# Where the third-block sums of the seventh up group stand in a Strassen-Winograd MLP: before or behind the second down unit's left sums

## Chip, core and metric

One core of one Trainium2 chip. The metric is device microseconds of one execution; the kernel before takes 881.0 us, the median of 3 runs (880.43 to 881.81). The engines are named as in the profile: PE (matrix products) with its weight loads PEld, DVE (elementwise), ACT (activations, copies, and a DMA queue of its own), POOL, and SP, which only issues DMAs.

## What is computed

Routing attention, then a squared-ReLU MLP on its output. In the reference, cut to what matters:

```
x = attn_out.transpose(0, 2, 1, 3).reshape(3072, 512)   # 4 batches of 768 tokens
h = x @ w_in                                            # 512 x 2048
r = np.maximum(h, 0.0)
g = r * r
return (g @ w_out).astype(np.float32)                   # 2048 x 512
```

The attention runs in about the first 320 us and the change does not touch it. Everything below is the MLP.

## The kernel before, in words

**Stages.** The MLP handles the 4 batches one after the other, as n = 0, 1, 2, 3. Each has an *up* part (x @ w_in, ReLU, square, giving the tile `g`) and a *down* part (g @ w_out). The loop that calls them is at L1409 ff.: n = 0 uses `first_up` and `first_down`; n = 1, 2, 3 use `up` (L890) and the class `Down` (L1122), whose `run` (L1255) writes the order of the work out by hand. No scheduler reorders it: every engine executes its own instructions in the order in which the program issues them, and so do the DMA queues of SP and ACT. An instruction that waits holds up all that is behind it on its engine.

**Fast products.** Both matrix products are done by a Winograd form of Strassen's scheme: seven products of half-size operands instead of eight, for which sums and differences of the operand blocks have to be made first. The sums of the left operand `g` are made by DVE. In `up`, the 16 row blocks of the hidden dimension are made in F2 = 8 groups (i = 0 to 7), each giving four blocks c11, c12, c21, c22 of `g`. The "seventh group" is i = F2 - 2 = 6, and the last is i = 7.

**Two kinds of sums of a finished group f.** A batch's 768 tokens are two halves of 3 blocks of 128.
- `first_level(g, f)` (L1088) makes the sums over the first two token blocks (columns `TWO`): a `plus` and two `sub` of 128x256. The down units of this batch use them.
- `third_sums(g, n, f)` (L1100) deals with the third token block (columns `THIRD`): a `plus` and three `sub` of 128x128 into a tile `third`, which a DMA then stores to `g_far[n]` in DRAM (L1109). For f < 7 it first calls `store_third` (L1095), which stores the third block's own parts of `g` by one or, for even n, two DMAs. The third blocks of two batches (0 with 1, 2 with 3) are multiplied together in the down part of the odd batch, which reads them back from `g_far` by `load_left` (L1147).

`up` calls these for each group a group or two after it is made. For the seventh group `first_level` runs in the last group, and its `third_sums` is the very last thing that `up` issues (L971-972); the closure that would store the `third` tile is put on a list. For the last group (f = 7) `first_level` is the first line of `Down.run`, and `third_sums` comes in the first unit.

**Units of the down part.** `Down.run` goes through 7 units (n = 2) or 14 (n = 1 and 3, the third blocks of two batches being units of their own, `of` = 1). A unit is one half-size product, itself done by seven quarter-size products (`times`, L1111), each of 4 matmuls into a slice of a PSUM bank. In the trace one such matmul shows as 2 records, so that a quarter product is a row of x8. In a unit u, in this order:
- six quarter products on PE; behind the first, an ACT copy (L1270), and for u = 0 the stores of L1272-1273 on ACT's queue
- on DVE: the first step of the combination of the unit before (none for u = 0); then `sub(x[0][1], x[0][1], s[:, 1])` (L1282), which overwrites a left block with a difference
- the seventh quarter product on PE (L1283), whose left operand is that difference
- `load_right` for the next unit (L1286; four DMAs on SP into the four slots of `home`, each of which waits until PE has read its slot)
- `parts` (L1293): DVE makes the left sums of unit u + 1: a `plus` and two `sub` of 128x512
- for u = 0: `third_sums` of the last group, the left loads, the store of `third`
- the second step of the combination of the unit before

`parts` of the first unit is called in `up` already (`behind_seven`, L945). So at the seam between up and down DVE has, in this order: the last adds and the square of group 7, `third_sums(6)`, `first_level(7)`, the difference of L1282, the left sums of the second unit, `third_sums(7)`.

Of the kernel before, what the change touches and what calls it, by code (L numbers as in the profile page):

```python
# [25 lines left out]
def kernel(  # L26
# [10 lines left out]
    nc = tc.nc  # L37
# [849 lines left out]
        plus(middle, c34, middle)  # L887
        yield

    def up(b, g, n, x, behind_seven, stores):  # L890
        flat = g.rearrange("p f h n -> p (f h n)")
        odd = n == B - 1
        w_next = w_sums(0, odd)
        lefts, rights, done = {}, {}, []
        for i in range(F2):
            w, w_next = w_next, w_sums(i + 1, odd) if i + 1 < F2 else None
            ((c11, c12), (c21, c22)), product = group(i, g, w, x)
            ends, late = i >= F2 - 2, i % 2

            def result(j):  # L900
                bank = bank_tile(TB)
                product(j, bank)
                return bank

            def add(j, *results):
                bank = result(j)
                for out, to in results:
                    plus(out, bank, to)

            def levels_1():  # L910
                if done:
                    first_level(g, done[0])

            def levels_2():
                if done:
                    third_sums(g, n, done.pop(0))()

            def two():
                add(2, (c11, c11))
                square(c11)  # L920
                if i < F2 - 1:
                    levels_2()

            if i < 2:
                nc.scalar.copy(out=c11, in_=result(1))
            elif not late:
                next(unit_1)
                if ends:
                    load_right(1)
            if not (late or ends):  # L930
                lefts[4] = second_lefts(4, i)
            add(6, (c12, c11))
            if i < F2 - 1:
                levels_1()
            if i == 1:
                rights[1] = second_rights(1, x[0][0][0])
            if not late or ends:
                two()
            if i == 0:
                rights[4] = second_rights(4, x[4])  # L940
            add(7, (c21, c12))
            if ends:
                levels_1()
            if i == F2 - 1:
                behind_seven()  # L945
            r = spare_tile.rearrange("p i n -> p (i n)")
            if late and not ends:
                unit_4 = second(lefts.pop(4), rights[4], r, 0, TB)
                next(unit_4)
            add(5, (c22, c21), (c12, c12))  # L950
            square(c22)
            if i == F2 - 2:
                levels_2()
            if ends:
                sub(c21, c21, result(4))
            elif late:
                next(unit_4)
                unit_1 = second(
                    second_lefts(1, i + 1), rights[1], flat, 2 * TB * (i + 1), 2 * TB
                )  # L960
                next(unit_1)
                both = g[:, F2 + i - 1 : F2 + i + 1, 0]
                sub(both, both, r.rearrange("p (i n) -> p i n", i=2))
                for k in range(2):
                    square(both[:, k])
                two()
            add(3, (c12, c12))
            if ends:
                square(c21)
            (square if i < F2 - 1 else square_by_dve)(c12)  # L970
            if i == F2 - 1:  # L971
                stores.append(third_sums(g, n, i - 1))
            done.extend([i] if ends else [i - 1, i] if late else [])
        xT.pop(b)

# [119 lines left out]
    def store_third(g, n, f, queue=nc.sync):  # L1095
        queue.dma_start(g_far[n][f, :, 1:3], g[:, F2 + f, :, THIRD])
        if n % 2 == 0:
            queue.dma_start(g_far[n][f, :, 0], g[:, f, 0, THIRD])

    def third_sums(g, n, f):  # L1100
        if f < F2 - 1:
            store_third(g, n, f)
        a = block_of(g, f, THIRD)
        third = outp.tile([P, DM], F32, name="third", tag="osb").rearrange("p (j n) -> p j n", j=4)
        plus(third[:, 0], a[1][0], a[1][1])
        sub(third[:, 1], third[:, 0], a[0][0])
        sub(third[:, 2], a[0][0], a[1][0])
        sub(third[:, 3], a[0][1], third[:, 1])
        return lambda queue=nc.sync: queue.dma_start(g_far[n][f, :, 3:7], third)  # L1109

    def times(bank, left, rhs):  # L1111
        for f in range(F4):
# [8 lines left out]

    class Down:  # L1122
        def __init__(self, b, g, n):
            self.up_stores = []
            self.b, self.g, self.n = b, g, n
            both = n % 2
            self.units = (
                [(0, 1), (0, 4), (1, 4), (1, 1)] if both else [(0, 1), (0, 4)]
            ) + [(of, j) for j in RIGHT_ORDER[2:] for of in range(1 + both)]
            a = blocks(g, TWO)  # L1130
            s1, s2 = (s_home(i) for i in range(2))
            self.lefts = {
                1: a[0][0], 2: a[0][1], 3: s1, 4: a[1][1], 5: s1, 6: s2, 7: a[1][0]
            }
            self.a, self.s1, self.s2 = a, s1, s2
            self.count = 0
            self.stores = []
# [117 lines left out]
        def run(self):  # L1255
            first_level(self.g, F2 - 1)
            waiting = None
            for u, (of, j) in enumerate(self.units):
                x, s = self.ahead
                y = quarters(right(j))  # L1260
                copied = spare_tile[:, 4 + u % 2]
                one, two = (
                    bank_tile(4 * P).rearrange("p (i n) -> p i n", i=4) for _ in range(2)
                )

                ends = self.n == B - 1 and u + 1 == len(self.units)
                five = bank_tile(P) if ends else two[:, 3]
                last = bank_tile(P) if ends else None
                times(one[:, 0], x[0][0], y[0][0])
                nc.scalar.copy(out=copied, in_=one[:, 0])  # L1270
                if u == 0:
                    store_third(self.g, self.n, F2 - 1, nc.scalar)  # L1272
                    self.up_stores.pop()(nc.scalar)
                self.store()
                times(two[:, 0], x[0][1], y[1][0])
                times(two[:, 1], s[:, 1], slot(1))
                times(two[:, 2], x[1][0], slot(2))
                times(five, s[:, 0], slot(0))
                times(one[:, 2], x[1][1], slot(3))
                if waiting:  # L1280
                    next(waiting)
                sub(x[0][1], x[0][1], s[:, 1])  # L1282
                times(last if ends else one[:, 1], x[0][1], y[1][1])  # L1283
                if u + 1 < len(self.units):
                    if (k := self.units[u + 1][1]) != j:
                        load_right(k)  # L1286
                    if of and j in LATER:
                        self.load_left(LATER[j])
                    if self.n % 2 and u == 2:
                        self.load_left(5)  # L1290
                    if self.units[u - 1] == (0, 5):
                        sub(self.s1, self.a[0][1], self.s2)
                    self.parts()  # L1293
                if u == 0:
                    store = third_sums(self.g, self.n, F2 - 1)
                    self.find_results()
                    if self.n % 2:
                        self.load_left(4)
                        self.load_left(1)
                    store()  # L1300
                if waiting:
                    next(waiting, None)
                waiting = self.combine(of, j, one, two, five, copied, last)
                to_end = len(self.units) - 1 - u
                for kk in LOADS[self.n % 2].get(u, ()):
                    load_x(self.n + 1, kk)
                if to_end == 2 - self.n % 2:
                    sum_x(self.n + 1, 1)
                elif to_end == 0:
                    sum_x(self.n + 1, 2)  # L1310
            if self.n == B - 1:
                self.store(nc.sync)
            list(waiting)
            sum_x(self.n + 1, 1)
            self.store()
# [79 lines left out]
    x_summed = {}  # L1395
# [8 lines left out]
    for n, b in enumerate(FEED):  # L1404
# [12 lines left out]
            )  # L1417
        else:
            stage = Down(b, g, n)
            up(b, g, n, x_summed.pop(n)[-1], stage.parts, stage.up_stores)  # L1420
            stage.run()
    manual.close()
    fast.close()
# [190 lines left out]
```

## Time and profile before

| what | us |
|---|---|
| median of 3 runs | 881.0 |
| the profiled execution | 880.63 |
| its span (first to last instruction) | 878.8 |
| outside its span | 1.83 |
| PE busy | 870.7 (99% of the span) |
| DVE busy | 755.9 (86%) |
| ACT busy | 385.9 (44%) |
| POOL busy | 182.4 (21%) |

Up and down of n = 1 meet at about 512 us, those of n = 2 at 670 us, and those of n = 3 at 784.5 us. The profile gives for each row the engine, the line of the kernel and the operation, out<-in by tile names, shape and count. A bracket such as [1.39 <-DVE g L551] says how long the engine had been idle and what released it. Rows of matmuls have modelled ends; the distance from one start to the next is the better measure of PE's pace. SPq and ACTq rows are DMA issues by those engines' queues. The granted clock of PE in the profiled execution is 0.999 of full speed.

### The profile page before, as it was taken

The page shows a single profiled execution, that of the slowest core. Times are in us where ns is not written, and L with a number is a line of the kernel's source. Part 1 is how long each engine was busy: PE and PEld are TensorE (multiplying, and loading weights), DVE is VectorE, ACT ScalarE, POOL GpSimd, SP SyncE. Part 2 cuts the span into 40 slices and gives each one's busy share as a digit, 9 for nine tenths or more (in the row PEclk, how much of TensorE's full clock was granted, in tenths as well). Part 3 has the DMA queues.
Part 4 walks back from the last instruction along what each step waited for, and adds up shares of the span by engine and source line. Part 5 has one row for each costly group of instructions (what it writes and reads, how often), then busy time and mean ns, then how long its engine had stood idle before and what let it go on. Part 6 is the DMA issues. An engine that isn't in the chain of part 4 may idle for free.

```text
span 878.8 us, 14998 instructions
## 1 busy us (share of the span) xinstructions
PE 870.7 (99%) x5487; PEld 597.9 (68%) x5487; DVE 755.9 (86%) x1359; ACT 385.9 (44%) x621; POOL 182.4 (21%) x240
## 2 busy tenths in 40 slices
PE   9999999999999999999999999999999999999997
PEld 5444444444444455568866689997767977769997
DVE  6799888888888999999859986797899898997786
ACT  5877667777765657750034420002543015440000
POOL 0000010000000236740055300005540064500000
PEclk9999999999999999999999999999999999999999
DMA  7777786866764235226701347681024730147563
GB/s 253 175 188 202 214 267 177 209 181 194 203 168 124 83 139 172 89 95 227 277 25 43 101 145 217 186 258 37 31 91 148 240 116 25 37 134 230 166 203 124
DMA packets 166402, 136.05 MB, mean 155 GB/s; under 512 B 58826, under 2 KB 140082, under 8 KB 166066
## 3 DMA queue, kind: packets, MB, share of 16 engines
q1 hardware_dynamic: 148546, 118.67, 45.7%
q10 hardware_dynamic: 17776, 16.36, 5.9%
q8 instruction: 45, 0.74, 0.3%
q14 instruction: 35, 0.29, 0.1%
HBM read 82.10 MB, written 41.89 MB: 141 GB/s over the span
## 4 chain that ended last, share of the span: by engine, by line
PE 98%; DVE 0%; DMA 0%; ACT 0%; issue 0%; DVEq 0%
PE bank L793 28%; PE bank L1113 25%; PE sc L441 14%; PE av_a L475 10%; PE bank L1005 6%; PE av_b L475 5%; PE sc L450 4%; PE bank L883 3%; PE sc L329 1%; PE more L883 1%; PE sc L494 1%; PE more L873 1%; DMA q_raw<-in_q_dram 0%; PE av_a L289 0%; ACT ex L457 0%; PE av_a L274 0%
## 5 line engine op out<-in xcount | busy, mean ns | idle before, releaser
L457 ACT ACTIVATE ex<-sc 128x1024 f32<-128x1024 f32 x144 | 144.4, 1026 | 37.5 <-PE sc L441 31.6
L441 PE MATMUL sc<-qkT 64*128 64x512 f32 (+1 forms) x768 | 150.5, 484 | 0.0
L990 DVE TENSOR_TENSOR g<-bank,g 128x384 f32<-128x384 f32 (+3 forms) x205 | 102.2, 515 | 21.1 <-PE bank L793 12.5
L769 ACT ACTIVATE g<-g 128x384 f32<-128x384 f32 x122 | 63.0, 516 | 96.5 <-DVE g L990 75.2
L441 PEld LDWEIGHTS sc<-qkT 64*128 64x128 f32 x768 | 65.6, 188 | 42.1 <-issue 30.2
L793 PE MATMUL bank<-xT,w_s 128*128 128x384 f32 x256 | 93.1, 486 | 0.0
L793 PE MATMUL bank<-x_t,w_s 128*128 128x384 f32 x256 | 93.0, 486 | 0.0
L1270 ACT COPY spare<-bank 128x128 f32<-128x128 f32 x35 | 9.3, 264 | 187.9 <-PE bank L1113 149.7
L475 PE MATMUL av_a<-ex,v_raw 128*64 128x512 f32 x384 | 85.9, 596 | 0.0
L460 DVE TENSOR_TENSOR total<-total,ex 128x1024 f32<-128x1024 f32 x64 | 78.7, 1229 | 6.5
L161 POOL TENSOR_TENSOR w_in<-w_in,w_raw 128x512 int32<-128x512 int32 x16 | 21.5, 1341 | 294.4 <-DVE w_in L153 294.4
L571 POOL TENSOR_TENSOR w_s<-w_in 128x256 f32<-128x256 f32 x32 | 26.3, 821 | 247.4 <-PE bank L1113 146.5
L1113 PE MATMUL bank<-home,l 128*128 128x128 f32 x560 | 74.0, 275 | 0.0
L793 PEld LDWEIGHTS bank<-xT,w_s 128*128 128x128 f32 x256 | 48.6, 190 | 34.3 <-issue 0.6
L1113 PEld LDWEIGHTS bank<-home,l 128*128 128x128 f32 x560 | 68.2, 192 | 0.0
L793 PEld LDWEIGHTS bank<-x_t,w_s 128*128 128x128 f32 x256 | 48.1, 190 | 29.1
L793 PE MATMUL bank<-xT,w_in 128*128 128x384 f32 x184 | 67.1, 487 | 0.0
L770 ACT ACTIVATE g<-g 128x384 f32<-128x384 f32 x122 | 63.8, 523 | 3.9
L475 PEld LDWEIGHTS av_a<-ex,v_raw 128*64 128x64 f32 x384 | 26.1, 137 | 51.0 <-issue 49.7
L450 PE MATMUL sc<-rows 64*128 64x512 bf16 (+1 forms) x360 | 58.8, 323 | 0.0
L793 PEld LDWEIGHTS bank<-xT,w_in 128*128 128x128 f32 x184 | 34.4, 190 | 21.7 <-DVE g L551 0.6
L1113 PE MATMUL bank<-home,g 128*128 128x128 f32 x352 | 46.5, 275 | 0.0
(221 smaller groups left out, 1560.6 us busy)
## 6 DMA issues: line engine op xcount, KB each, us to landing
home<-w_far SPq DMA_DIRECT2D x92, 256.0 KB
words<-flat SPq DMA_DIRECT2D x26, 384.0 KB
w_raw<-in_moe_w_in_dram SPq DMA_DIRECT2D x16, 512.0 KB
w_raw<-in_moe_w_out_dram SPq DMA_DIRECT2D x16, 512.0 KB
w_far<-home SPq DMA_DIRECT2D x28, 256.0 KB
g<-g_far SPq DMA_DIRECT2D x28, 256.0 KB
v_raw<-in_v_dram SPq DMA_DIRECT2D x16, 384.0 KB
rb<-far_r SPq DMA_DIRECT2D x30, 192.0 KB
```

What stands on the lines that cost most here:

```text
L441: nc.tensor.matmul(sc[i][:, e, cols], lhsT=qkT[pair][rows, NCH + c], rhs=qkT[pair][rows, n.start // P : n.stop // P], start=first, stop=no ...
L450: nc.tensor.matmul(sc[i][:, e, cols], lhsT=ohT[pair][rows, 1, c * P : (c + 1) * P], rhs=ohT[pair][rows, 0, columns(i)], start=first, stop= ...
L457: nc.scalar.activation(out=ex[i], in_=sc.pop(i), func=ACT.Exp, scale=SCALE)
L460: eng.tensor_tensor(out=out, in0=a, in1=b, op=ALU.add)
L475: nc.tensor.matmul(bank[D * e : D * (e + 1), 0 : n.stop - n.start], lhsT=raw_v[pair][:, e, c], rhs=ex[i][:, e, cols], start=c == 0, stop=c ...
L769: nc.scalar.activation(out=to, in_=to, func=ACT.Relu)
L770: nc.scalar.square(to, to)
L793: nc.tensor.matmul(bank, lhsT=operands[j][0][:, kk], rhs=operands[j][1][:, kk], start=(kk == 0), stop=(kk == H2 - 1),)
L883: nc.tensor.matmul(bank, lhsT=left, rhs=right, start=True, stop=True)
L990: nc.vector.tensor_tensor(out=out, in0=one, in1=two, op=ALU.add)
L1005: nc.tensor.matmul(bank, lhsT=left[j][:, f], rhs=right(j)[:, f], start=(f == 0), stop=(f == F2 - 1),)
L1113: nc.tensor.matmul(bank, lhsT=left[:, f], rhs=rhs[:, f], start=(f == 0), stop=(f == F4 - 1))
```

## The change

```diff
-    def up(b, g, n, x, behind_seven, stores):
+    def up(b, g, n, x, behind_seven):
 ...
             (square if i < F2 - 1 else square_by_dve)(c12)
-            if i == F2 - 1:
-                stores.append(third_sums(g, n, i - 1))
             done.extend([i] if ends else [i - 1, i] if late else [])
 ...
     def third_sums(g, n, f):
-        if f < F2 - 1:
+        if f < F2 - 2:
             store_third(g, n, f)
 ...
-        return lambda queue=nc.sync: queue.dma_start(g_far[n][f, :, 3:7], third)
+        return lambda: nc.sync.dma_start(g_far[n][f, :, 3:7], third)
 ...
                 if u == 0:
-                    store_third(self.g, self.n, F2 - 1, nc.scalar)
-                    self.up_stores.pop()(nc.scalar)
+                    for f in (F2 - 2, F2 - 1):
+                        store_third(self.g, self.n, f, nc.scalar)
 ...
                 if u == 0:
-                    store = third_sums(self.g, self.n, F2 - 1)
+                    stores = [third_sums(self.g, self.n, f) for f in (F2 - 2, F2 - 1)]
                     self.find_results()
                     if self.n % 2:
                         self.load_left(4)
                         self.load_left(1)
-                    store()
+                    for store in stores:
+                        store()
```

In each of n = 1, 2, 3:
- On DVE the four instructions of `third_sums(6)` leave their place behind the square of group 7 and stand behind the left sums of the second unit, right ahead of the four of `third_sums(7)`. Nothing else moves on DVE.
- On ACT's queue the store of the sums of group 6 (256 KB) is gone; the stores of the third block's own parts of group 6 (128 KB, for n = 2 also 64 KB) are new, ahead of those of group 7.
- On SP's queue those stores of group 6 are gone from the end of `up`, and the 256 KB store of its sums is new, just ahead of the store of group 7's sums; for n = 1 and 3 both stand behind the left loads of L1298-1299.

PE's and POOL's instructions and their order are the same as before. The work done is the same in number and kind; one list and one argument go away.

More of the change, by code (lines that the diff above doesn't have):

```diff
@@ L1123, in __init__ @@
         def __init__(self, b, g, n):
-            self.up_stores = []
             self.b, self.g, self.n = b, g, n
@@ L1419 @@
             stage = Down(b, g, n)
-            up(b, g, n, x_summed.pop(n)[-1], stage.parts, stage.up_stores)
+            up(b, g, n, x_summed.pop(n)[-1], stage.parts)
             stage.run()
```

## The prediction

> **What bounds the kernel now.** I read the page's busy times first, then who waited for whom, then the chain that ended last from 700 us on, then the timeline at the three seams between up and down.
>
> The busy table and PE's waits in the whole MLP:
>
> ```profile
> PE 870.7 (99%) x5487; PEld 597.9 (68%) x5487; DVE 755.9 (86%) x1359; ACT 385.9 (44%) x621; POOL 182.4 (21%) x240
> ```
> ```profile
> PE bank L1113 <- DVE g L551: 1.4, 1, 1.4
> ```
>
> PE is the bound. Only what closes a gap in PE's stream can shorten the run, and the waits show just one gap in the MLP: 1.4 us, for a DVE subtraction. The chain shows where it lies, at the seam of n = 3 (start, us, what):
>
> ```profile
> 784.52 2.69 PE bank L1113 x24
> ...
> 787.21 0.56 DVE g L990
> ...
> 787.80 0.56 DVE g L773
> 788.36 0.21 DVE third L990
> ...
> 788.59 0.69 DVE third L551 x3
> 789.28 0.35 DVE home L990
> ...
> 790.52 0.70 DVE g L551
> 791.22 0.04 issue
> 791.27 82.47 PE bank L1113 x736
> ```
>
> Between the square of group 7 (L773) and `first_level(7)` (the "home" step) lie the four instructions that the change takes out. Behind them comes the difference of L1282 (790.52), which PE's seventh quarter product needs. From 791.27 to the end the chain is PE alone.
>
> Now the same place in the timeline, n = 3 and then n = 1:
>
> ```profile
> 788.27 0.28 DVE L990 TENSOR_TENSOR third<-g 128x128 f32<-128x128 f32 x1
> ...
> 788.82 1.06 PE L1113 MATMUL bank<-home,g 128*128 128x128 f32 x8
> ...
> 789.20 0.42 DVE L990 TENSOR_TENSOR home<-g 128x256 f32<-128x256 f32 x1
> ...
> 791.27 1.16 PE L1113 MATMUL bank<-w_out,g 128*128 128x128 f32 x8 [1.39 <-DVE g L551]
> ```
> ```profile
> 515.67 1.06 PE L1113 MATMUL bank<-home,l 128*128 128x128 f32 x8
> ...
> 516.56 1.06 PE L1113 MATMUL bank<-home,g 128*128 128x128 f32 x8
> 516.67 0.69 DVE L551 TENSOR_TENSOR g<-g,l 128x512 f32<-128x512 f32 x1
> ...
> 517.46 1.12 PE L1113 MATMUL bank<-w_out,g 128*128 128x128 f32 x8
> ```
>
> Quarter products start 0.892 us apart (786.14, 787.03, 787.92, 788.82 in n = 3). The seventh of n = 3 should start at 789.71 and starts at 791.27, so PE really loses 1.56 us (the row's 1.39 counts from a modelled end). In n = 1 it starts on time, at 517.46, but its weight loads start 0.96 us behind the ones before instead of 0.89: the difference ends at 517.36, just about when PE wants it. The loss is 0.07 us. The rows of n = 2 (675.47 behind 674.58, loads at 675.42 behind 674.47) give the same 0.07. So all that waits for DVE at the three seams is 1.56 + 0.07 + 0.07 = 1.70 us.
>
> **The four DVE instructions leave their place.** In n = 3 they reach from 788.27 to 789.20, start to next start: 0.93 us. Not all of that comes back. The first of them starts at 788.27, while the square before it (787.80, 0.56 long) still runs until 788.36; it doesn't depend on it. `first_level(7)` reads the square's result, and where one DVE instruction needs the one before it, the rows show a start 0.03 to 0.04 us behind its end (789.20 + 0.42 = 789.62, next 789.66). So it will start at 788.40, not at 788.27. It also waits for ACT's square of c22, done at 787.49. The gain is 789.20 - 788.40 = 0.80 us, not 0.93. Here the Trainium skill speaks otherwise: "VectorE: DVE Perf Modes", section "The DRAIN you can't avoid", says that each DVE instruction waits until the pipe is empty anyway, and that a semaphore between them costs nothing extra. By that rule order would not matter and the whole 0.93 would return; by the row a dependent start costs 0.13 us more than an independent one. I take the row: 0.80.
>
> The difference then ends at 790.41 instead of 791.21, and PE's seventh product starts at 790.47. **n = 3 gains 0.80**, and 0.76 of the stall stays; the same instruction is still what PE waits for. **n = 1 and n = 2 gain their 0.07 each**, all they have. The sum is 0.80 + 0.07 + 0.07 = **0.94 us**.
>
> **Where they go.** Behind the left sums of the second unit, DVE now has eight instructions of third-block sums instead of four. Those left sums end 0.80 earlier, so the first group stands in the hole: it starts near 792.26 (793.06 less 0.80) and the second group near 793.19 instead of 793.06, 0.13 late. Behind it stand the first combination (794.23 before, after 0.16 idle) and the difference of unit 1 (795.36 to 796.05). PE wants that difference at 791.27 + 7 x 0.892 = 797.51 before, and at 796.71 after. It should be there by about 796.0, so 0.7 us are spare and the cost is nothing. Without that cover, a delay d of DVE costs d - 0.7. In n = 1 and n = 2 the spare time is larger by the stall that they don't have there. From unit 2 on DVE waits for PE again (2.18 us at 806.76), so lateness doesn't pile up.
>
> Can the eight be slow there? The trace has slow ones: the group of n = 3 at 769.34 has instructions of 0.82 us instead of 0.28, beside sums on POOL that take 1.29 instead of 0.73 at 767.17. The Trainium skill ("SBUF — State Buffer", section "SBUF: two separate sides") calls the port pair that VectorE and GpSimd share an exclusive lock, which the loser waits for. By that rule, with POOL busy, a group would cost up to 4 x 0.82 = 3.3 us in place of 0.93, and the change would lose 1.7 us. But POOL's busy time is 0.00 from 784 to 800 us, and its next stage's sums wait for PE in the down part (93.9 us in n = 1). I take 0.93.
>
> **The queues.** SP loses the stores of group 6's own parts (781.77 in n = 3) and gains one 256 KB store. For odd n it stands behind the left loads, an issue of 0.5 us at 795.6 with SP idle until 801.39: nothing. For n = 2 the two stores go out at about 677.9 and 678.4, and `load_right` behind them is held by PE until 679.29 anyway; 256 KB at the 317 GB/s seen there is 0.8 us more traffic, while slot 1 is wanted at 678.21 + 6.25 = 684.46 and three microseconds are there. ACT's queue loses the wait for `third` (issue at 789.32) and gets one or two stores of 0.4 to 0.5 us; its next copy is due at 793.36, so 3 us cover that. The second left load at 794.10 overwrites what group 6's store still reads, so that store, now issued at 788.5 instead of 781.77, must have landed. The profile has that load wait 1.2 us for such a store (from about 790.7, so landed by 791.9) and then 2.2 us for `third_sums(7)`. One store more ahead moves 791.9 to 792.4, and the sums still come last. Bounds: zero gain, since nothing waits for an earlier issue, and at most 0.5 us of lateness. I take zero.
>
> Against the profiled execution: 880.63 - 0.94 = 879.69. The median of the runs is 0.37 above that execution, so 881.0 - 0.94 = **880.1**.
>
> **Rivals.** *A, more is hidden in the stalls.* The other executions may have DVE later at the seams than the profiled one, since the slow groups beside POOL vary (two slow instructions in n = 1, three in n = 3). n = 1 and n = 2 sit exactly on the edge, so any lateness there returns in full up to 0.80: at most 3 x 0.80 = 2.4, or 878.6; the 0.37 of the median alone would make it 879.7. Against it: 1.43 us of lateness that the profile doesn't show would have to be there. *B, the gain is given back.* The margin of 0.7 at unit 1's difference is used up, if the eight instructions or the copy before the combination come later than worked out. Then PE loses at unit 1 what it won at unit 0, and 880.9 results (the 0.14 of n = 1 and n = 2 remains). The row of the combination, which waited for PE and not for DVE, speaks against it. *C, slower: the second left load of the odd stages lands late*, because it now waits for a store issued 7 us later on another queue. It is wanted at 799.40 - 0.80 = 798.60 in n = 3; before, traffic restarts at 795.2 and its 256 KB are over by about 796.4. It decides if the load comes more than 2.2 us later, and makes the kernel slower in all from about 3 us; at 3.5 us n = 3 loses 1.3, n = 1 (3.1 of margin) 0.4, less the 0.94: 881.8. Against it is the wait for `third_sums(7)`, which comes after that store by nearly 2 us. That the change does not do what it says can be left out: the order of the instructions on DVE shows exactly the move.
>
> **Chances.** The forecast 0.60, A 0.22, B 0.12, C 0.06. A measurement of this kernel tells about 0.2% (1.8 us) from no change; 0.94 is 0.11%. Over that bound on the fast side lies about two thirds of A and a little scatter: 0.18. On the slow side half of C and scatter: 0.05. Within: 0.77. The range takes in most of A and all of B, with the runs' own scatter of 0.7: 878.9 to 881.2.
>
> **What would show it.** Right: at the seam of n = 3 the "home" row follows the square directly, about 0.04 us behind its end; PE's wait for "DVE g L551" falls from 1.39 to about 0.6; loads in n = 1 and n = 2 start 0.89 apart; the eight "third" rows stand together at about 0.28 each; no new wait on PE in units 1 and 2. Wrong: "third" rows of 0.8, a PE wait at unit 1's seventh product (B), or PE waiting for a DMA at the start of unit 2 (C); or a wait at that seam that has not changed, because DVE came to it later from the up part.

## The result

| | us, median | runs | lowest and highest |
|---|---|---|---|
| before | 880.64 | 17 | 879.89 to 881.81 |
| changed | 879.16 | 17 | 878.18 to 879.86 |

The ratio is 0.9982, interval 0.9975 to 0.9988: 1.48 us faster, and from 1.1 to 2.2 by the interval. The forecast was 0.94 us, to 880.1 (counted from the 880.64 measured here, 879.7); the range held the time. The sum was too small, and the profile shows where. The profiled execution of the changed kernel took 878.45 us, its span 876.7.

The busy table and the list of what PE waited for (us in total, times, longest):

```profile
PE 869.9 (99%) x5487; PEld 597.4 (68%) x5487; DVE 754.3 (86%) x1359; ACT 385.8 (44%) x621; POOL 181.7 (21%) x240
```
```profile
PE sc L179 <- DVE zeros L176: 1.1, 1, 1.1
PE av_a L274 <- DMA q_raw<-in_q_dram: 0.3, 1, 0.3
```

PE's wait for DVE at the seam is not smaller, it is gone; the two waits left are at the very start of the kernel. The chain that ended last now runs from the third seam to the end without a break (784 records in one piece, 736 and 24 with DVE between them before):

```profile
768.32 15.48 PE bank L793 x48
783.80 87.56 PE bank L1111 x784
```

The seam itself in the timeline of the changed kernel, n = 3 and then n = 1. L1111 is L1113 of before, L988 is L990:

```profile
783.64 1.95 PE L1111 MATMUL bank<-w_out,g 128*128 128x128 f32 x16
...
785.48 0.56 DVE L773 SCALAR_TENSOR_TENSOR g<-g 128x384 f32<-128x384 f32 x1
...
786.14 0.42 DVE L988 TENSOR_TENSOR home<-g 128x256 f32<-128x256 f32 x1
...
787.47 0.69 DVE L551 TENSOR_TENSOR g<-g,l 128x512 f32<-128x512 f32 x1
...
788.10 1.06 PE L1111 MATMUL bank<-home,g 128*128 128x128 f32 x8
...
789.00 1.06 PE L1111 MATMUL bank<-w_out,g 128*128 128x128 f32 x8
```
```profile
515.96 1.06 PE L1111 MATMUL bank<-home,g 128*128 128x128 f32 x8
...
516.86 1.06 PE L1111 MATMUL bank<-w_out,g 128*128 128x128 f32 x8
```

`first_level(7)` follows the square, as it should. In n = 3 the square starts 1.84 us behind PE's first down product (785.48 against 783.64). Before, it was 3.45 us: the square at 787.80, and PE's row

```profile
784.35 1.95 PE L1113 MATMUL bank<-w_out,g 128*128 128x128 f32 x16
```

So DVE came to the seam 1.6 us earlier *before it reached a single instruction that the change moves*. The difference of L1282 ends at 788.16, 0.8 us ahead of its use at 789.00.

### The profile page after: what moved, and what is told of

Its sections match the earlier page's. It is cut to its first block, busy times and chain, and to the rows that moved or that the text cites. A ratio compares the mean times of both kernels' runs of the same rounds, so it can differ in the third digit from the quotient of the medians.

```text
span 876.7 us, 14996 instructions
## 1 busy us (share of the span) xinstructions
PE 869.9 (99%) x5487; PEld 597.4 (68%) x5487; DVE 754.3 (86%) x1359; ACT 385.8 (44%) x621; POOL 181.7 (21%) x240
## 4 chain that ended last, share of the span: by engine, by line
PE 99%; DMA 0%; ACT 0%; DVE 0%; issue 0%
PE bank L793 28%; PE bank L1111 25%; PE sc L441 14%; PE av_a L475 10%; PE bank L1003 6%; PE av_b L475 5%; PE sc L450 4%; PE bank L883 3%; PE sc L329 1%; PE more L883 1%; PE sc L494 1%; PE more L873 1%; DMA q_raw<-in_q_dram 0%; PE av_a L289 0%; ACT ex L457 0%; PE sc L274 0%
## 5 line engine op out<-in xcount | busy, mean ns | idle before, releaser
L988 DVE TENSOR_TENSOR g<-bank,g 128x384 f32<-128x384 f32 (+3 forms) x205 | 102.3, 515 | 21.1 <-PE bank L793 12.8
L1111 PE MATMUL bank<-home,l 128*128 128x128 f32 x560 | 74.0, 275 | 0.0
L1111 PEld LDWEIGHTS bank<-home,l 128*128 128x128 f32 x560 | 68.2, 192 | 0.0
L1111 PE MATMUL bank<-home,g 128*128 128x128 f32 x352 | 46.5, 275 | 0.0
```

Source lines behind the costliest of these rows:

```text
L988: nc.vector.tensor_tensor(out=out, in0=one, in1=two, op=ALU.add)
L1111: nc.tensor.matmul(bank, lhsT=left[:, f], rhs=rhs[:, f], start=(f == 0), stop=(f == F4 - 1))
```

## Where DVE lost 1.6 us before, and why it no longer does

Followed back through the up part of n = 3, the traces first part in its group 3. Before, DVE stands idle for 0.46 us between two adds; with only the stores moved (`stores_only`, below) it is idle there for 0.10. The kernel before, then that one, whose second add is shown once more alone:

```profile
744.32 0.54 DVE L990 TENSOR_TENSOR g<-bank,g 128x384 f32<-128x384 f32 x1
745.32 1.02 DVE L990 TENSOR_TENSOR g<-bank,g 128x384 f32<-128x384 f32 x2 [0.46 <-PE bank L883]
```
```profile
744.31 1.67 DVE L990 TENSOR_TENSOR g<-bank,g 128x384 f32<-128x384 f32 x3
...
744.96 0.56 DVE L990 TENSOR_TENSOR g<-bank,g 128x384 f32<-128x384 f32 x1
```

From one add to the next it is 1.00 us before and 0.65 in stores_only, so DVE is 0.35 us late from there on. The bracket names PE, but PE's rows of the two kernels lie within 0.02 us of each other here, and in stores_only the same add starts 0.35 us sooner: PE is not what it waited for.

The 0.35 us grow in the next third-block sums. In the kernel before POOL starts first, in the changed kernel DVE does:

```profile
749.72 0.73 POOL L571 TENSOR_TENSOR w_s<-w_in 128x256 f32<-128x256 f32 x1 [1.73 <-PE bank L793]
...
749.89 0.70 DVE L990 TENSOR_TENSOR third<-g 128x128 f32<-128x128 f32 x1
...
750.63 0.78 DVE L551 TENSOR_TENSOR third<-third,g 128x128 f32<-128x128 f32 x1
```
```profile
748.82 0.28 DVE L988 TENSOR_TENSOR third<-g 128x128 f32<-128x128 f32 x1
749.00 0.73 POOL L571 TENSOR_TENSOR w_s<-w_in 128x256 f32<-128x256 f32 x1 [1.74 <-PE bank L793]
...
749.13 0.75 DVE L551 TENSOR_TENSOR third<-third,g 128x128 f32<-128x128 f32 x1
...
749.81 0.28 DVE L551 TENSOR_TENSOR third<-g 128x128 f32<-128x128 f32 x1
```

On time, DVE gets every second sum through between POOL's: 2 of 4 take 0.28 us. Late by 0.35, it meets POOL's sums in all four, and they take 0.70 to 0.82. Counted in the timeline, the up part of n = 3 has 8 sums of 0.6 us or more before (four in group 3, one in group 4, three in group 5) and 4 after (two each in groups 3 and 5). Row against row, DVE's delay against stores_only grows from 0.37 to 1.35 us in the sums of group 3 and to 1.89 with the one slow sum of group 4. It falls to 1.27 where stores_only is slowed in its turn, is back at 1.89 after group 5, and 1.61 at the seam. That is what turns 0.35 us into 1.6 us.

## The experiments

The table comes from each kernel's profile: slow sums (0.6 us or more) in the up part of n = 3, and the stall of PE at the third seam, which is the start of the seventh product less where four more steps of 0.892 put it. The ratio is to runs of the kernel before on the same chip. Slow sums and stalls are read from one profile of each kernel.

| kernel | us | ratio, interval | slow sums, n = 3 | third stall |
|---|---|---|---|---|
| before_again | 880.75 | 1.0001 (0.9993 to 1.0009) | 8 | 1.57 |
| sums_only | 879.22 | 0.9988 (0.9978 to 0.9998) | 4 | 0.00 |
| stores_only | 879.13 | 0.9982 (0.9976 to 0.9988) | 4 | 0.00 |
| double_seam | 883.55 | 1.0033 (1.0020 to 1.0046) | 4 | 0.89 |
| nudge_third | 879.56 | 0.9985 (0.9978 to 0.9992) | 4 | 0.00 |
| nudge_first | 879.60 | 0.9988 (0.9981 to 0.9994) | 4 | 0.01 |
| late_sums_first | 880.66 | 1.0000 (0.9992 to 1.0009) | 4 | 1.51 |
| late_sums_moved | 879.84 | 0.9991 (0.9983 to 1.0000) | 4 | 0.77 |
| pause_sums_first | 881.03 | 1.0002 (0.9994 to 1.0010) | 8 | 1.56 |
| pause_sums_moved | 880.09 | 0.9995 (0.9986 to 1.0004) | 8 | 0.84 |
| nudge_changed | 879.46 | 0.9984 (0.9977 to 0.9991) | 4 | 0.00 |
| after_again | 879.21 | 0.9981 (0.9974 to 0.9987) | 4 | 0.00 |

**Theories.** D: DVE's work at the seam delays PE one to one wherever DVE is late. Q: the gain comes from the queues. L: the third stall is an unlucky timing of DVE in the up part, which the change happens to break. A: a pause of half a microsecond is enough to start it.

**before_again**: no edit.

> The kernel before, unchanged, profiled once more. Theory D (DVE is late at the seam, and the stall comes back one to one where PE waits): the time is that of before, ratio 1.000 within 0.001, and the third seam again shows a stall of about 1.56 us. Theory L (the extra half microsecond of the gain, and the size of the third stall, is luck of how DVE meets POOL in the up part, different in every execution): the same time, but the third stall differs from 1.56 us by half a microsecond or more, together with the number of third-block sums of 0.7 us and more in the up part of n = 3 (7 or 8 in the first profile).

The pause is there again (745.43, 0.46 us), so are the 8 slow sums, and the stall is 1.57. So, as far as two profiles can tell, the lateness isn't drawn anew in each execution, as L had it: it belongs to this kernel.

**sums_only** and **stores_only** split the change.

```diff
 sums_only, against the changed kernel
+            if i == F2 - 1:
+                store_third(g, n, i - 1)
 ...
-                    for f in (F2 - 2, F2 - 1):
-                        store_third(self.g, self.n, f, nc.scalar)
+                    store_third(self.g, self.n, F2 - 1, nc.scalar)
```

> Only the four DVE instructions of group 6 move behind the second unit's left sums, and the store of their result with them; the stores of the third block's own parts of group 6 stay at the end of up on SP. Theory D: all of the gain, ratio 0.998 to 0.9985, no PE wait at the seams of n = 1 and n = 2. Theory Q (the gain comes from the queues: SP is free earlier, ACT waits for nothing): little or none of it, ratio 0.9995 to 1.000.

```diff
 stores_only, against before
-        if f < F2 - 1:
+        if f < F2 - 2:
 ...
-                    store_third(self.g, self.n, F2 - 1, nc.scalar)
-                    self.up_stores.pop()(nc.scalar)
+                    for f in (F2 - 2, F2 - 1):
+                        store_third(self.g, self.n, f, nc.scalar)
 ...
+                    self.up_stores.pop()()
                     store()
```

> Only the stores move, as in the change (group 6's own parts to ACT's queue, the store of the sums to SP behind the left loads); the four DVE instructions stay behind the square of group 7. Theory D: no gain, ratio 0.9995 to 1.0005, the third stall as in before. Theory Q: the gain of the change, ratio 0.998 to 0.9985.

*Each half gives about the whole gain.* D alone is wrong about stores_only, and Q alone about sums_only, whose third stall is gone too. By the medians the halves give 1.6 and 1.7 us, where both together give 1.5. (By its ratio sums_only gives 1.1 us, 0.2 to 1.9 by the interval; its time alone does not refute Q.) So the halves have something in common. What they share is in the table: 4 slow sums, no pause, no third stall. (They also share one edit, the store of group 6's sums on SP's queue; it is not the cause, since nudge_third below loses the stall without it and pause_sums_first has the stall with it.) In stores_only the four instructions still stand ahead of `first_level(7)`, and PE does not mind, because DVE is 1.6 us earlier. The difference between the halves is small: the down part of n = 1 is one piece of 87.54 us in sums_only and 87.61 in stores_only, that of n = 2 43.77 and 43.83. So the moved instructions are worth 0.07 and 0.06 us where DVE is on time, as forecast.

**double_seam**: the four instructions of group 6 made twice at their old place.

```diff
+        for _ in range(2 if f == F2 - 2 else 1):
             plus(third[:, 0], a[1][0], a[1][1])
 ...
```

> The kernel before with the four DVE instructions of group 6 made twice, into the same tile with the same values, at the place where they stand before the change. Theory D: DVE is 0.93 us later at each seam; n = 1 and n = 2 sit on the edge and n = 3 behind it, so PE loses about 0.9 us three times, 2.6 to 2.8 us in all, 883.3 us, ratio 1.003. Theory Q: at most 0.3 us, ratio 1.000. If only n = 3 were late in an ordinary execution, 0.9 us.

2.7 us slower than before, as D had it, though not as D laid it out. PE's waits:

```profile
PE bank L1114 <- DVE g L551: 3.8, 3, 2.3
```

By the starts, the three stalls are 0.89, 2.50 and 0.89. In n = 1 and n = 3 that is the doubled group on a DVE that is on time. In n = 2 there is 1.6 more, and 8 slow sums, behind a pause for which the bracket names DVE itself, not PE:

```profile
634.73 0.56 DVE L990 TENSOR_TENSOR spare<-more,spare 128x384 f32<-128x384 f32 x1 [0.47 <-DVE spare L990]
```

So with this edit the lateness is gone from n = 3 and stands in n = 2. D holds for the price of seam work; L holds in that the lateness falls elsewhere.

**nudge_third** and its control **nudge_first**: one tiny DVE copy in the up part, nothing at the seam.

```diff
+            if n == 3 and i == 3:        # nudge_first: n == 1
+                nc.vector.tensor_copy(out=flag_spare, in_=ups[:, 0:1])
             add(5, (c22, c21), (c12, c12))
```

> The kernel before with one more DVE instruction, a copy of one element per partition into an unused tile, in the up part of n = 3, group 3, ahead of the add of the fifth product; nothing at the seam is changed. In both profiles of the kernel before, DVE waits 0.46 us at that add and comes late from there on (8 slow third-block sums against 4), and in no other kernel so far. Theory L (the third stall is made by that wait, and anything that shifts DVE against PE by a few hundredths of a microsecond removes it): the 0.46 us wait is gone, 4 slow sums, the third stall falls from 1.56 to about 0.1 us, 879.2 us, ratio 0.998 to 0.9985. Theory D alone (the stall is the DVE work at the seam): no change or 0.1 us more, ratio 1.000.

> The control: the same extra copy at the same place of the up part of n = 1. Theory L in the narrow sense (only the phase in n = 3 matters): n = 3 as in before, ratio 1.000. Theory L in the wide sense (any small edit ahead of it draws a new phase): the wait may vanish here too, or appear in another stage; then the ratio is 0.998 to 0.9985 and the profile shows 4 slow sums in n = 3.

Both lose the third stall and gain 1.3 us by the medians, with 4 slow sums. Extra work in DVE makes the kernel faster, and the control in n = 1 acts on n = 3 too. That is L in its wide sense, but not by a shift in time. In nudge_third:

```profile
744.96 0.55 DVE L992 TENSOR_TENSOR g<-bank,g 128x384 f32<-128x384 f32 x1
745.43 0.14 DVE L951 COPY flag_spare<-ups 128x1 f32<-128x1 f32 x1
745.61 1.02 DVE L992 TENSOR_TENSOR g<-bank,g 128x384 f32<-128x384 f32 x2
```

The copy fits into the usual step: 0.65 us from add to add, as in stores_only, which has no copy. What it does change is the number that each later instruction has in DVE's stream (see the pause, below).

**late_sums_first** and **late_sums_moved** make DVE late by extra sums of group 5 in n = 3, in stores_only and in the changed kernel. They measure what the prediction worked out: the moved sums' worth with a late DVE.

```diff
+        for _ in range(3 if n == 3 and f == 5 else 1):
             plus(third[:, 0], a[1][0], a[1][1])
 ...
```

> The stores are placed as in the change, the DVE instructions of group 6 as before it, and DVE is made late on purpose: in the up part of n = 3 the four third-block sums of group 5 are made three times (same tile, same values), 1.86 us more work of which about 0.3 fills an idle stretch. Theory D: the third seam stalls by about 1.6 us, so 1.5 us more than with the stores alone, 880.6 to 880.7 us, ratio to before 1.000. Theory Q (the gain is the stores): 879.2 us, ratio 0.998.

> The changed kernel with the same delay of DVE in the up part of n = 3. Theory D, with the numbers of the prediction: the third seam stalls by 0.76 us instead of 1.56, 0.80 us less than the run with the sums first, and n = 1 and n = 2 give 0.07 each: 879.7 to 879.9 us, ratio 0.999. If a DVE instruction at the seam did not cost PE anything, both delayed kernels would take the same time.

PE's waits, the sums first and then moved:

```profile
PE bank L1114 <- DVE g L551: 1.3, 1, 1.3
```
```profile
PE bank L1112 <- DVE g L551: 0.6, 1, 0.6
```

The stall falls from 1.51 to 0.77, by 0.74, and the medians lie 0.82 apart. The runs of the two overlap (880.15 to 881.96 and 879.08 to 881.10), so the stall is the sharper measure. This is the forecast's step, in the situation that the forecast assumed.

**pause_sums_first** and **pause_sums_moved** put a delay of that size back by hand, three additions of 64 columns where DVE had paused. Both have the stores as in the change; the first has the sums at their old place. The edit that they share:

```diff
+            if n == 3 and i == 3:
+                for _ in range(3):
+                    plus(flag_spare, ups, ups)
             add(5, (c22, c21), (c12, c12))
```

> The stores as in the change, the DVE instructions of group 6 as before it, and three small extra DVE additions (64 columns, into an unused tile), about 0.5 us together, ahead of the add of the fifth product in group 3 of the up part of n = 3: there DVE paused by 0.46 us in the kernel before. Theory A (the pause alone starts the lateness, because the next third-block sums then begin after POOL's sums instead of ahead of them and all four are slowed, in group 3 and again in group 5): 8 slow sums in n = 3 instead of 4, a third stall of about 1.6 us, 880.7 us, ratio to before 1.000. If a pause of half a microsecond only delays DVE by itself: 4 slow sums, a stall of at most 0.5 us, 879.2 to 879.7 us.

> The changed kernel with the same three small additions. Theory A with theory D: 8 slow sums in n = 3, and a third stall of 0.77 us, as in the run that was made late in group 5; 879.9 us, ratio 0.999. Without the amplification: no stall, 879.2 us.

```profile
744.22 0.55 DVE L993 TENSOR_TENSOR g<-bank,g 128x384 f32<-128x384 f32 x1
744.69 0.72 DVE L993 TENSOR_TENSOR flag_spare<-ups 128x64 f32<-128x64 f32 x3
745.33 1.01 DVE L993 TENSOR_TENSOR g<-bank,g 128x384 f32<-128x384 f32 x2
```

The additions delay the add by 0.46 us (it starts 1.11 us behind the add before it, where 0.65 is usual; in the kernel before it was 1.00). With the sums first, the whole picture of the kernel before is back: 8 slow sums, a stall of 1.56, its time. The first sum again starts behind POOL's:

```profile
749.91 0.60 DVE L993 TENSOR_TENSOR third<-g 128x128 f32<-128x128 f32 x1
```

With the sums moved the stall is 0.84, 0.72 less, and the medians are 0.94 apart. A is shown: 0.46 us at this place is enough, and the 0.35 of the kernel before made the same stall.

**nudge_changed** puts the tiny copy into the changed kernel, and **after_again** is the changed kernel once more.

> The changed kernel with the one small copy that removed the third stall from the kernel before. Theory L (the copy only takes the lateness of n = 3 away, which the changed kernel doesn't have): as the changed kernel, 879.2 us, no stall at the third seam; against the kernel before with the copy, which has its sums at the old place, 0.2 to 0.4 us less. Rival: the copy itself costs 0.3 us wherever it is, then 879.5 us.

> The changed kernel, unchanged, profiled once more. Theory L: 4 slow sums in n = 3 again, no pause in DVE, no stall of PE at any seam, 879.2 us, ratio 0.998. If the phase is drawn anew in each execution: a pause and a stall of 0.77 us at one of the seams are possible.

after_again agrees with L: no pause, no stall. nudge_changed has no stall either. Its time lies between the forecast and the rival, and 0.1 us below nudge_third where 0.2 to 0.4 was expected; with intervals of 0.0014 (1.2 us) these runs can't tell a few tenths apart, and what the copy itself costs stays open. In before_again, nudge_third and pause_sums_first PE also waits once for a load of `home`, 0.15 to 0.24 us at 812 to 813; two of these have no copy.

## The prediction, step by step

- *PE is the bound and only the seam stalls are to be had, 1.70 us:* right, and exhausted. All three are gone.
- *The moved instructions are worth 0.80 us at a late seam:* right in kind, 0.74 and 0.72 measured. The term that was off is the dependent start. I took 0.04 us between the square and `first_level(7)`; it is 0.10 in the changed kernel (786.04 to 786.14) and 0.11 in late_sums_moved. The rows that I took 0.04 from have one wait; this instruction waits for DVE and for ACT. The row of before with two waits, for DVE and for PE, had it: the difference of L1282 starts 0.10 behind the end of its predecessor (790.42, 790.52). The rule of the Trainium skill ("VectorE: DVE Perf Modes", "The DRAIN you can't avoid"), that a semaphore between DVE instructions costs nothing extra, is off here by more than I allowed: an instruction that does not wait for the one before it starts 0.08 us ahead of that one's profiled end, one with two waits 0.10 behind it. The same section adds that a next instruction that is not held back starts earlier, which the prediction left out.
- *n = 1 and n = 2 gain 0.07 each:* right (87.60 to 87.54, 43.83 to 43.77).
- *"0.76 of the stall stays":* this step failed. 0.00 stayed. I carried DVE's lateness at the third seam over from the profile of before, as if the up part of n = 3, which the change doesn't touch, had to run the same. It came from a pause that every edit tried here moves or hides, the change among them; that the forecast's sum lay as near as 0.94 to 1.48 is luck. Where lateness is put back by hand, 0.77 and 0.84 do stay. With 1.56 for 0.80 the sum is 1.70; the two profiles differ from the first seam to the end of the span by 1.58 (366.74 and 365.16), the medians by 1.48.
- *Rival A* looked to stalls in n = 1 and n = 2 that the profile doesn't show; there were none. It noted slow sums in one group, two in n = 1 and three in n = 3; over the whole up part they are 4 and 8, and that was the mark of the lateness. (Its 1.43 us is 1.46, 2.40 less 0.94.) *B* and *C* did not happen: no PE wait in units 1 and 2. The queues were not quite free, though. In one profile of the changed kernel `load_right` of the third seam took 3.64 us to issue instead of 3.00, and DVE waited 0.24 us for the first left load, not the second:

```profile
794.51 0.69 DVE L551 TENSOR_TENSOR l<-l,g 128x512 f32<-128x512 f32 x1 [0.24 <-DMA g<-g_far]
```

DVE had the time; in after_again that wait is absent.
- *The eight sums at the new place take 0.28 each, POOL being idle:* right (0.28 to 0.29 in the changed kernel's third seam). The 1.7 us of loss set against this counted one group of sums and left out the gain. I weighed the rule of the Trainium skill on the port that DVE and POOL share ("SBUF — State Buffer", "SBUF: two separate sides") only there. The collisions that agree with it, 0.70 to 0.82 us for 0.28, decided the result 40 us earlier.

So the kernel is faster by what was hoped for, but the move as such is not what the 1.48 us show. On a DVE that is on time it is worth about 0.2 us in all, which these runs can't resolve. Its worth of 0.7 us is insurance for a seam to which DVE comes late.

**Where the pause falls.** Its place follows from a count. Beside its 1359 instructions DVE has semaphore records in the trace (EVENT_SEMAPHORE, 401 in the kernel before), which the timeline does not print. With these counted in order of start, the add that pauses is DVE's record 1472 in both profiles of the kernel before, and record 1216 in double_seam, 256 earlier. Each stands right behind a semaphore record and starts 0.40 to 0.41 us after it, where 0.06 is the median. Three other profiles have the same pause at record 1600, 128 later, in the third-block sums at the seam, where it did no harm (nudge_third, nudge_first, pause_sums_first; this is nudge_first):

```profile
792.96 0.29 DVE L551 TENSOR_TENSOR third<-g,third 128x128 f32<-128x128 f32 x1 [0.26 <-DVE third L551]
```

Over all 14 profiles an instruction stands right behind a semaphore record at number 64, or at 64 plus a multiple of 128, in 22 places, and at none of them does it start less than 0.39 us after it. In the profiles without the pause in an up part, record 1472 is itself a semaphore record, or an instruction with none right ahead of it. So, by this count, an edit that adds or takes away one DVE record anywhere ahead moves the pause to another instruction, often to one where it doesn't show. That is how a copy in n = 1 can act on n = 3, and stores alone too: stores_only has 1763 DVE records, before 1765, the changed kernel 1766, with the same 1359 instructions.

**What stays open** is why there is a pause at these numbers. Within 1 us behind each of the six clear ones begins a transfer of 8 KB on a queue that the page lists as "instruction", so waiting for instructions is a candidate; but such transfers also begin where no pause shows. No run was made to test the count, for instance with 1 and with 128 more DVE instructions ahead.

## What to carry to other kernels

When an engine is late at a place where the bound engine waits, follow it back to the first row at which two traces part, before the delay is taken as given; it may come from where the instructions happen to stand in an engine's stream, which any edit shifts, and then every edit looks like a gain. Split a change into halves: if each half gives all of it, look for what the halves share. To price a step that works against lateness, bring the lateness about in both versions, and compare those (0.82 and 0.94 us here by the medians, 0.74 and 0.72 by the stalls).

## What the runs showed that was not expected

- A delay of 0.35 us in DVE became 1.6 us, because four sums of 0.28 us fell behind a row of POOL sums of 0.73 us instead of in front of it, and met more of them in the next two groups as well. One extra DVE copy of 0.14 us, in a place where it delays nothing, made the kernel 1.3 us faster.
- The lateness is a property of the program, not of the execution, as far as these profiles go: in two profiles each of two kernels it is there both times, or not at all. The pause that starts it falls on numbers in DVE's stream that are 128 or 256 apart.
